# Pooled attention and a top-1 mixture of experts on one core: the turns of K and V put ahead of a unit's products with V

## The chip, the cores and the metric

The program runs on one core of one Trainium2 chip. The metric is the device time of one execution in microseconds (us). Before the change three runs took 642.44, 642.95 and 644.0 us, median 642.95. A core has five engines with a queue of its own each: TensorE (PE, with its weight loads shown as PEld), VectorE (DVE), ScalarE (ACT), GpSimd (POOL) and SyncE (SP), which starts most of the transfers.

## The reference, cut to what matters

q, k and v have 8 batches, 8 heads, 576 rows and 64 columns. K and V are averaged over groups of 8 rows, so a head has 72 pooled rows. The result of attention feeds a router and a layer of 8 experts:

```python
k_p = k.reshape(B, H, Sp, pool, D).mean(axis=3)
v_p = v.reshape(B, H, Sp, pool, D).mean(axis=3)
scores = scale * np.matmul(q, k_p.transpose(0, 1, 3, 2))
attn = softmax(scores)
x = (attn @ v_p) -> rows of 512        # 4608 rows
logits = x @ w_gate                    # 8 experts, the best one is taken
y[i] = gate_w[i] * (relu(x[i] @ w1[e]) @ w2[e])   # up to 1152 rows of each expert
```

## The kernel before, in words

The kernel has two stages. **Attention** takes up to about 193 us of the trace; a loop over pairs of row tiles through the experts follows. The change lies in attention alone.

Attention is cut into 36 **units**: 128 pairs of query rows for 4 heads at a time (`class Unit`, L438). One pass of the loop at L1011, called iteration n here (0 to 37), works on three units at once. It computes the scores of unit n (`score`, L472: `ps`), subtracts the row maximum on DVE (`softmax`, L479 and L484) and takes the exponential on ACT (`exp`, L487: `pt`). For unit n-2 it turns the exponentials in two halves on TensorE (`p_t`, L495: `pp`), copies each half on ACT (L496: `pT`) and multiplies with V (`av`, L509: `pa`), and DVE divides by the sums (`norm`, L518 to L549: `rz`, `xo`, `lt`, `lg`). For unit n+1 it turns the query rows (`q_part`, L455 and L456: `pq`, `qT`). A unit with neither of the extra works below takes some 3.6 us of TensorE.

Extra work is spread over the iterations. Two batches make a pair of nine units, and in each pair K and V of the two batches are prepared:

- **K's turn** (`prep_k`, called by `hooks` where j, the place in the pair, is 1 or 5): five transposes on TensorE (L404: `pk`), then four copies on ACT (L413) into `kbs`, about 1.75 us.
- **V's turn** (first part of `prep_v`, one iteration later): five transposes (L404) and two copies on ACT (L413) into `vT`.
- **V's product** (second part of `prep_v`, a further iteration later): twelve rows of matmuls on TensorE (L431: `pv`) with an identity and the router's weights, then two multiplications on DVE (L433 and L435) into `vbd`, the operand that `av` uses.
- **Early rows** (`transposed`, L836, iterations 31 and 32): 256 rows of the first expert are turned on TensorE (L840: `pxe`) and split into a high and a low part on ACT and DVE (L125 and L126).
- The **router's steps** (`route`, L577: `gmx`, `gd`, `gme`, `oh`, `su`, `po`, `gps` and so on) run one by one on DVE between the steps of a norm.
- POOL adds up the pooled rows of the next pairs (`tree`, L368 to L372) and later scatters row numbers (L672) and computes low parts of weights (L126).

What sets the order: every engine runs its instructions in the order in which the Python code writes them (`tc.manual_schedule`, L732). There is no planner; queues of generators (`hq` for V's preparation, `rq` for routing, `gq` and `sq` for POOL) are advanced by `step` at fixed places of the loop. `hooks(n)` stands at the end of an iteration, behind the norm.

Two facts on space matter. All small PSUM tiles (`pp`, `pq`, `pk`, `pv`, `pxe`, `po`) come from `bank` (L173), which hands out two banks in turn; a tile waits until the readers of the tile before it in its bank are done. In an iteration the order of the calls is `pp`, `pp`, `pq`, and then a turn's tile, which so takes the bank of the second `pp`. And `pa` has one buffer, so the products of a unit wait for the norm of the unit before.

Iteration 1 is special: V's turn and V's product of the first batch both stand there, with five filler matmuls (`busy`, L262) ahead of them.

Of the kernel before, what the change touches and what calls it, by code (L numbers as in the profile page):

```python
# [21 lines left out]
P = 128  # L22
KC = 96
# [8 lines left out]
def pooled_attn_top1_moe(ctx: ExitStack, tc: tile.TileContext, q, k, v, wg, w1, w2, cap, out):  # L32
# [8 lines left out]
    B, H, S, D = q.shape  # L41
    NT, DM = out.shape
    E, _, DF = w1.shape
    POOL = 8
    SP_ = S // POOL
    NCH = H * SP_ // KC
# [10 lines left out]
    NR = 9  # L57
# [66 lines left out]
    def split(hi, lo, src, eng=nc.vector):  # L124
        nc.scalar.copy(hi, src)  # L125
        eng.tensor_sub(lo, src, hi.bitcast(F32))  # L126
# [35 lines left out]
    with ExitStack() as actx:  # L162
# [10 lines left out]
        def bank(shape, name, dtype=F32):  # L173

            turn[0] ^= 1
            return ptp.tile(shape, dtype, name=name, tag=f"tp{turn[0]}")
# [45 lines left out]
        raws, qb, qtl, kps, vps, left = {}, {}, {}, {}, {}, {}  # L222
# [39 lines left out]
        def busy(n, z=None):  # L262

            z = bank([P, 512], "z") if z is None else z
            for _ in range(n):
                nc.tensor.matmul(z[:, 0:P], zw, zw, start=True, stop=True)  # L266
            return z
# [95 lines left out]
        def tree(dst, t, due=None):  # L363

            n = t.shape[1]
            t1 = kvp.tile([P, NR // 3, W // 2], F32, name="t1", tag="t1", bufs=1)[:, 0:n]
            t2 = kvp.tile([P, NR // 3, W // 4], F32, name="t2", tag="t2", bufs=1)[:, 0:n]
            nc.gpsimd.tensor_add(t1, t[:, :, 0 : W // 2], t[:, :, W // 2 :])  # L368
            yield
            nc.gpsimd.tensor_add(t2, t1[:, :, 0 : W // 4], t1[:, :, W // 4 :])  # L370
            yield
            nc.gpsimd.tensor_add(dst, t2[:, :, 0:D], t2[:, :, D:])  # L372
            if due:
                left[due] -= 1
            yield

        def red(dst, t):
            nc.vector.tensor_reduce(out=dst, in_=t.rearrange("p c (j d) -> p c d j", j=POOL), axis=AX.X, op=ALU.add)

        def pooled(p):  # L380

            kps[p] = kvp.tile([P, NR, D], F32, name="kp", tag="kp", bufs=2)
            vps[p] = kvp.tile([P, NR, D], F32, name="vp", tag="vp", bufs=2)

        def third(i):
            return slice(i * NR // 3, (i + 1) * NR // 3)

        def pool(p):
            for w, dst in (("k", kps[p]), ("v", vps[p])):
                left[w, p] = 3  # L390
                for i in range(3):
                    gq.append(tree(dst[:, third(i)], raws[p]["kv".index(w)][i], (w, p)))
# [15 lines left out]
        def natural(dst, pk):  # L408

            v = dst.rearrange("d h (g r) -> d (h g) r", r=NR)  # L410
            for o in range(2):
                n = (NR + 1 - o) // 2
                nc.scalar.copy(v[:, :, o : NR : 2], pk[o * D : (o + 1) * D, 0 : n * GB].rearrange("d (i q) -> d q i", q=GB))  # L413
# [8 lines left out]
        def prep_v(b):  # L422

            vT = wk.tile([D, H, SP_], F32, name="vT", tag="vT", bufs=1)
            natural(vT, turned(vps[b // 2], b, "v"))
            yield
            vb = vbd[b % 2]
            rows_ = vT.rearrange("d h x -> d (h x)")
            pv = bank([P, 512], "pv")[0:KC, 0 : NCH * (D + 2 * E)].rearrange("r (c x) -> r c x", c=NCH)
            for c in range(NCH):  # L430
                nc.tensor.matmul(pv[:, c], rows_[:, c * KC : (c + 1) * KC], wgi[:, c], start=True, stop=True)  # L431
            m = mk[:, :, :, None]
            nc.vector.tensor_mul(vb[:, :, :, D : D + E], pv[:, :, D:].rearrange("r c (a e) -> r c a e", a=2),  # L433
                                 m.to_broadcast([KC, NCH, 2, E]))
            nc.vector.tensor_mul(vb[:, :, :, 0:D], pv[:, :, None, 0:D].to_broadcast([KC, NCH, 2, D]), m.to_broadcast([KC, NCH, 2, D]))  # L435
            yield
# [123 lines left out]
        first, lgs, rows_out, early = {}, {}, [], {}  # L560
# [129 lines left out]
        rq, hq, aq, dq, sq, gq = [], [], [], [], [], []  # L690
# [26 lines left out]
        def step(q_, n=1):  # L717

            while q_ and n:
                if callable(q_[0]):  # L720
                    q_.pop(0)()
                    n -= 1
                elif next(q_[0], 0) == 0:
                    q_.pop(0)
                else:
                    n -= 1

        def drain(q_):
            while q_:
                step(q_)  # L730

        with tc.manual_schedule():  # L732
# [28 lines left out]
            n_early = nu - 11  # L761
# [74 lines left out]
            def transposed(i, x):  # L836

                p_ = bank([P, KD, P], "pxe", F32R)
                for c in range(KD):
                    nc.tensor.transpose(p_[:, c], x[:, i, c * P : (c + 1) * P], identr)  # L840
                s = (slice(None), slice(None), slice(i * P, (i + 1) * P))
                split(xh[s], xl[s], p_.bitcast(F32))
# [130 lines left out]

            NPU = 2 * NB + 1

            def hooks(n):

                p, j = divmod(n, NPU)
                if n == 0:
                    red(vps[0][:, NR - 1 :], raws[0][1][2][:, 2:3])  # L980
                    pooled(1)
                    pool(1)
                elif n == 1:
                    busy(5)
                    hq.append(prep_v(0))
                    drain(hq)
                if p == B // 2:
                    return
                if j == 1:
                    prep_k(2 * p + 1)  # L990
                if j == 2:
                    hq.append(prep_v(2 * p + 1))
                if p + 1 < B // 2:
                    if j == 5:
                        prep_k(2 * p + 2)
                    if j == 6:
                        hq.append(prep_v(2 * p + 2))

                if p + 2 < B // 2:
                    if j == (5 if p == 0 else 3):  # L1000
                        load_kv(p + 2)
                    if j == (7 if p == 0 else 6):
                        pooled(p + 2)
                        pool(p + 2)
                step(hq)
                if n == NB:
                    gq.append(rest)
                if n == 3 * NB:
                    setup_rows()

            for n in range(nu + 2):  # L1011
                u = units[n] if n < nu else None
                p = units[n - 2] if n > 1 else None
                nx = units[n + 1] if n + 1 < nu else None
                new = n and u and u.b != units[n - 1].b
                if new:
                    assert not aq
                    ahead(u.b)
                if n == n_start:
                    start_weights()  # L1020
                if n == n_early:
                    start_early()
                if n == n_early + 3:
                    start_ids()
                    split_early()
                if n == n_early + 4:
                    start_rows()
                if u:
                    u.score(0)
                if p:  # L1030
                    p.p_t(0)
                if u:
                    u.score(1)
                    u.softmax()
                step(aq)
                if p:
                    p.p_t(1)
                if n == nu + 1:
                    for c in range(KF):
                        nc.scalar.copy(wr["h"][:, c], wr[2][:, c])  # L1040
                if nx:
                    nx.q_part()
                flush()
                step(aq)
                if u:
                    u.exp()
                if p:
                    p.open()
                    p.av(0)
                    p.av(1)  # L1050
                step(rq, 4 if nu // 2 < n < nu - 8 else 8 if n >= nu - 8 else 0)
                step(dq)
                if p:
                    p.norm()
                    r = route_of(p)
                    if r:
                        rq.append(r)
                        if p.b == early_b - 1:
                            rq.append(favourite())
                if n_early + 6 <= n < n_early + 8:  # L1060
                    transposed(n - n_early - 6, early["x"])
                hooks(n)
                step(gq, 4 if n < n_early + 3 else max(0, min(2, n - n_early - 3)) + (n == n_start - 1))
                step(sq, 2 if n < nu - 10 else 4)
                step(aq)
# [135 lines left out]
```

## Time and profile before

| | us |
|---|---|
| runs, median (lowest to highest) | 642.95 (642.44 to 644.0) |
| the profiled execution | 645.5 |
| its span, first to last instruction | 643.8 |
| TensorE busy, weight loads | 614.2, 552.1 |
| DVE, ACT, POOL busy | 337.2, 235.0, 302.6 |
| mean granted TensorE clock | 0.991 |

A row of a timeline has the start and the duration in us, the engine, the line of the kernel, the operation, the output and its inputs, the sizes and how many instructions are merged; in brackets stands how long the engine was idle before it and whom it waited for. A row of the groups has the count, then the busy time and the mean ns of one, then the idle time before them. TensorE's rows overlap, since matmuls are pipelined; the distance of two starts is what a group takes.

### The profile page before, as it was taken

How to read it: one execution, taken by the hardware profiler on the slowest of the kernel's cores; microseconds unless marked ns; L12 is line 12 of the kernel's file. 1: busy time of each engine (PE TensorE's matmuls, PEld its weight loads, DVE VectorE, ACT ScalarE, POOL GpSimd, SP SyncE). 2: the span in 40 equal slices, each digit the busy share in tenths (PEclk: the TensorE clock that was granted, in tenths of full speed). 3: DMA queues.
4: the chain of work that ended last, by engine and by line, in shares of the span. 5: the costliest groups of instructions: out<-in, count | busy, mean ns of one | idle time of the engine just before them, and what ended most of it. 6: DMA issues, size and time to landing. Idle time of an engine off the chain costs nothing.

```text
span 643.8 us, 14831 instructions
## 1 busy us (share of the span) xinstructions
PE 614.2 (95%) x4241; PEld 552.1 (86%) x4242; DVE 337.2 (52%) x725; ACT 235.0 (36%) x398; POOL 302.6 (47%) x467
## 2 busy tenths in 40 slices
PE   9899899999979999998999999999999989999994
PEld 8789789888779889987989989988899878989983
DVE  4667878868778322267447732227422575322222
ACT  1665556557643211156235511116111462112111
POOL 7599939532953322425445532434434155441344
PEclk9999999999989999998999999999999999999998
DMA  8998744462172610227727650212712171210112
GB/s 327 356 403 280 286 156 122 169 202 96 67 290 75 228 34 33 65 90 261 274 81 280 208 185 33 65 33 95 255 49 65 51 269 36 65 49 19 63 49 65
DMA packets 47084, 93.81 MB, mean 146 GB/s; under 512 B 13392, under 2 KB 23632, under 8 KB 47060
## 3 DMA queue, kind: packets, MB, share of 16 engines
q1 hardware_dynamic: 30836, 60.37, 27.2%
q0 software_dynamic: 11392, 21.57, 11.0%
q10 hardware_dynamic: 4832, 11.56, 4.7%
q8 instruction: 14, 0.23, 0.1%
q14 instruction: 10, 0.08, 0.0%
HBM read 132.97 MB, written 31.27 MB: 255 GB/s over the span
## 4 chain that ended last, share of the span: by engine, by line
PE 83%; DVE 7%; issue 4%; ACT 2%; DVEq 2%; POOL 1%; POOLq 0%; ACTq 0%
PE y L159 29%; PE ph L150 24%; PE pa L509 7%; PE ps L472 4%; PE pp L495 3%; PE ph L1115 3%; PE pq L455 2%; PE z L266 2%; PE px L1092 2%; PE ps L150 1%; ACT kbs L413 1%; PE pv L431 1%; PE pa L159 1%; PE ps L159 1%; PE pk L404 1%
## 5 line engine op out<-in xcount | busy, mean ns | idle before, releaser
L1104 ACT ACTIVATE hh<-ph 128x512 fp32r<-128x512 f32 x60 | 35.9, 599 | 171.5 <-PE ph L150 168.4
L1105 DVE SCALAR_TENSOR_TENSOR hl<-ph,hh 128x512 fp32r<-128x512 f32 x60 | 40.9, 690 | 109.0 <-ACT hh L1104 96.7
L150 PE MATMUL ph<-xh,w1h 128*128 128x256 f32 x480 | 76.3, 281 | 1.6 <-ACT xo L957 0.8
L150 PE MATMUL ph<-xh,w1l 128*128 128x256 f32 x480 | 75.9, 280 | 0.0
L150 PE MATMUL ph<-xl,w1h 128*128 128x256 f32 x480 | 75.9, 280 | 0.0
L159 PE MATMUL y<-w2h,hh 128*128 128x512 f32 x280 | 72.5, 401 | 0.8 <-issue 0.8
L95 POOL DMA_INDIRECT xg<-xs,ix x42 | 43.9, 1046 | 56.9 <-PE y L159 49.6
L159 PE MATMUL y<-w2l,hh 128*128 128x512 f32 x280 | 69.9, 392 | 0.0
L159 PE MATMUL y<-w2h,hl 128*128 128x512 f32 x280 | 69.3, 390 | 0.0
L150 PEld LDWEIGHTS ph<-xh,w1h 128*128 128x128 f32 x480 | 65.7, 189 | 3.7 <-ACT xo L957 1.2
L509 PE MATMUL pa<-vbd,pT 96*128 96x146 f32 (+1 forms) x480 | 61.1, 290 | 4.3 <-DVE lt L535 2.6
L150 PEld LDWEIGHTS ph<-xl,w1h 128*128 128x128 f32 x480 | 65.2, 190 | 0.0
L150 PEld LDWEIGHTS ph<-xh,w1l 128*128 128x128 f32 x480 | 64.8, 189 | 0.0
L159 PEld LDWEIGHTS y<-w2l,hh 128*128 128x128 f32 x280 | 53.2, 190 | 11.3
L159 PEld LDWEIGHTS y<-w2h,hl 128*128 128x128 f32 x280 | 52.6, 188 | 10.9
L100 POOL DMA_INDIRECT out_dram<-zrow,iz x40 | 53.4, 1335 | 16.8 <-issue 14.7
L509 PEld LDWEIGHTS pa<-vbd,pT 96*128 96x128 f32 (+1 forms) x480 | 55.5, 179 | 6.4 <-DVE lt L535 3.3
L159 PEld LDWEIGHTS y<-w2h,hh 128*128 128x128 f32 x280 | 50.3, 189 | 11.1 <-issue 1.9
L126 DVE TENSOR_TENSOR xl<-px,xh 128x512 fp32r<-128x512 f32 x40 | 25.7, 685 | 60.5 <-ACT xh L125 60.5
L93 POOL TENSOR_TENSOR guard<-ix 128x2 int32<-128x2 int32 x21 | 5.5, 263 | 101.6 <-DVE ix L90 85.9
L672 POOL DMA_INDIRECT slots<-pairs,gix x36 | 35.3, 981 | 30.2 <-DVE pairs L665 10.8
L496 ACT COPY pT<-pp 96x384 f32<-96x384 f32 x72 | 34.1, 475 | 39.8 <-PE pp L495 34.5
(234 smaller groups left out, 1050.0 us busy)
## 6 DMA issues: line engine op xcount, KB each, us to landing
r<-in_moe_w_dram SPq DMA_DIRECT2D x84, 1024.0 KB
raw<-in_k_dram SPq DMA_DIRECT2D x12, 768.0 KB
raw<-in_v_dram SPq DMA_DIRECT2D x12, 768.0 KB
xs<-xo ACTq DMA_DIRECT2D x16, 512.0 KB
qblk<-in_q_dram SPq DMA_DIRECT2D x14, 512.0 KB
raw<-in_moe_w_dram SPq DMA_DIRECT2D x4, 512.0 KB
r<-in_moe_w_dram ACTq DMA_DIRECT2D x2, 1024.0 KB
qblk<-in_q_dram SPq DMA_DIRECT2D x4, 256.0 KB
```

What stands on the lines that cost most here:

```text
L95: nc.gpsimd.indirect_dma_start(out=dst[:, i, :].bitcast(F32), out_offset=None, in_=src, in_offset=bass.IndirectOffsetOnAxis(ap=ix[:, i, 0: ...
L100: ins = nc.gpsimd.indirect_dma_start(out=out[:, :], out_offset=bass.IndirectOffsetOnAxis(ap=i_, axis=0), in_=src, in_offset=None, bounds_c ...
L126: eng.tensor_sub(lo, src, hi.bitcast(F32))
L150: nc.tensor.matmul(p[:, f2], a[:, c, f * P : (f + 1) * P], b[:, c], start=(f2 == 0 and j == 0 and c == 0), stop=(f2 == 1 and j == 2 and c ...
L159: nc.tensor.matmul(y, a[:, c, i * P : (i + 1) * P], b[:, c], start=(n == 0), stop=(n == 3 * KF - 1))
L472: nc.tensor.matmul(self.ps[:, h, 0 : 2 * SP_].rearrange("p (a x) -> p a x", a=2), self.qT[:, h], kbs[self.b % 2][:, :, self.hf * HH + h], ...
L495: nc.tensor.transpose(pp[0:KC, c], self.pt[:, (j * HC + c) * KC : (j * HC + c + 1) * KC], ident)
L496: nc.scalar.copy(self.pT[:, j], pp[0:KC, 0:HC])
L509: nc.tensor.matmul(self.pa[us, j, h0 * XW : (h0 + 2) * XW], self.pT[:, j, c, us], vbd[b % 2][:, cc].rearrange("r a x -> r (a x)"), start=( ...
L672: ins = nc.gpsimd.indirect_dma_start(out=slots[:, :], out_offset=bass.IndirectOffsetOnAxis(ap=ix[:, g, 0:1], axis=0), in_=pairs[:, pr + g0 ...
L1104: nc.scalar.activation(hh[s], p, AF.Relu)
L1105: nc.vector.scalar_tensor_tensor(out=hl[s], in0=p, scalar=0.0, in1=hh[s].bitcast(F32), op0=ALU.max, op1=ALU.subtract)
```

## The change

A new function `turns(n)` takes K's turn, V's turn, V's product and the early rows out of the end of the iteration (out of `hooks`, behind the norm) and puts them between the exponential and the products with V. Loads and POOL's work stay in `hooks`. In iteration 1 the fillers and V's turn go ahead of the exponential, and four more fillers go ahead of V's first product, into its bank.

```diff
@@ prep_v
-            pv = bank([P, 512], "pv")[0:KC, 0 : NCH * (D + 2 * E)].rearrange("r (c x) -> r c x", c=NCH)
+            pv = bank([P, 512], "pv")
+            if b == 0:
+                busy(4, pv)
+            pv = pv[0:KC, 0 : NCH * (D + 2 * E)].rearrange("r (c x) -> r c x", c=NCH)
@@ the loop's helpers
-            def hooks(n):
+            def turns(n):
 
                 p, j = divmod(n, NPU)
-                if n == 0:
-                    red(vps[0][:, NR - 1 :], raws[0][1][2][:, 2:3])
-                    pooled(1)
-                    pool(1)
-                elif n == 1:
-                    busy(5)
-                    hq.append(prep_v(0))
+                if n == 1:
                     drain(hq)
+                if n_early + 6 <= n < n_early + 8:
+                    transposed(n - n_early - 6, early["x"])
                 if p == B // 2:
                     return
                 if j == 1:
...
                         prep_k(2 * p + 2)
                     if j == 6:
                         hq.append(prep_v(2 * p + 2))
-
+                step(hq)
+
+            def hooks(n):
+
+                p, j = divmod(n, NPU)
+                if n == 0:
+                    red(vps[0][:, NR - 1 :], raws[0][1][2][:, 2:3])
+                    pooled(1)
+                    pool(1)
+                if p == B // 2:
+                    return
                 if p + 2 < B // 2:
...
-                step(hq)
                 if n == NB:
@@ the loop
                 step(aq)
+                if n == 1:
+                    busy(5)
+                    hq.append(prep_v(0))
+                    step(hq)
                 if u:
                     u.exp()
+                turns(n)
                 if p:
                     p.open()
                     p.av(0)
...
-                if n_early + 6 <= n < n_early + 8:
-                    transposed(n - n_early - 6, early["x"])
                 hooks(n)
```

Line numbers of the changed kernel are higher by 3 from `prep_v`'s matmuls to `hooks`, and more behind it. TensorE, iterations 10 and 11, K's turn and V's turn. Before (`pa` is the product with V, `ps` the scores, `pp` the turned weights):

```order
L455 MATMUL pq<-identr,qblk 128x128 x4
L509 MATMUL pa<-vbd_149,pT 128x146 x6
L404 MATMUL pk<-identr,kp 128x64 x4
L404 MATMUL pk<-identr,kp 64x64
L472 MATMUL ps<-kbs_146,qT 128x144 x2
L495 MATMUL pp<-identr,pt 96x128 x3
L472 MATMUL ps<-kbs_146,qT 128x144 x2
L495 MATMUL pp<-identr,pt 96x128 x3
L455 MATMUL pq<-identr,qblk 128x128 x4
L509 MATMUL pa<-vbd_148,pT 128x146 x6
L404 MATMUL pk<-identr,vp 128x64 x4
L404 MATMUL pk<-identr,vp 64x64
```

And now:

```order
L458 MATMUL pq<-identr,qblk 128x128 x4
L404 MATMUL pk<-identr,kp 128x64 x4
L404 MATMUL pk<-identr,kp 64x64
L512 MATMUL pa<-vbd_149,pT 128x146 x6
L475 MATMUL ps<-kbs_146,qT 128x144 x2
L498 MATMUL pp<-identr,pt 96x128 x3
L475 MATMUL ps<-kbs_146,qT 128x144 x2
L498 MATMUL pp<-identr,pt 96x128 x3
L458 MATMUL pq<-identr,qblk 128x128 x4
L404 MATMUL pk<-identr,vp 128x64 x4
L404 MATMUL pk<-identr,vp 64x64
L512 MATMUL pa<-vbd_148,pT 128x146 x6
```

Each turn has moved ahead of the products with V of its own iteration. DVE, iteration 12, where V's product is multiplied into `vbd` and routing steps (`oh`, `su`) stand among the norm. Before:

```order
L484 TENSOR_TENSOR pt<-ps,mx 128x4x2x72
L518 TENSOR_SCALAR rz<-pa 128x8
L610 TENSOR_TENSOR oh_180<-cw,gmm 128x8
L520 RECIPROCAL rz<-rz 128x8
L614 TENSOR_REDUCE su<-oh_180 128x80
L534 TENSOR_TENSOR xo<-pa,rz 128x2x256
L535 TENSOR_TENSOR lt<-pa,rz 128x2x32
L621 TENSOR_REDUCE oh_181<-oh_180 128x8
L549 TENSOR_REDUCE lg<-lt 128x16
L433 TENSOR_TENSOR vbd_149<-pv,mk 96x12x8
L435 TENSOR_TENSOR vbd_149<-pv,mk 96x12x64
L479 TENSOR_REDUCE mx<-ps 128x8
```

And now:

```order
L487 TENSOR_TENSOR pt<-ps,mx 128x4x2x72
L436 TENSOR_TENSOR vbd_149<-pv,mk 96x12x8
L438 TENSOR_TENSOR vbd_149<-pv,mk 96x12x64
L521 TENSOR_SCALAR rz<-pa 128x8
L613 TENSOR_TENSOR oh_180<-cw,gmm 128x8
L523 RECIPROCAL rz<-rz 128x8
L617 TENSOR_REDUCE su<-oh_180 128x80
L537 TENSOR_TENSOR xo<-pa,rz 128x2x256
L538 TENSOR_TENSOR lt<-pa,rz 128x2x32
L624 TENSOR_REDUCE oh_181<-oh_180 128x8
L552 TENSOR_REDUCE lg<-lt 128x16
L482 TENSOR_REDUCE mx<-ps 128x8
```

The two multiplications have moved from behind the norm to ahead of it. DVE, iteration 31, the split of the early rows (`xl`). Before:

```order
L484 TENSOR_TENSOR pt<-ps,mx 128x4x2x72
L518 TENSOR_SCALAR rz<-pa 128x8
L520 RECIPROCAL rz<-rz 128x8
L534 TENSOR_TENSOR xo<-pa,rz 128x2x256
L535 TENSOR_TENSOR lt<-pa,rz 128x2x32
L126 TENSOR_TENSOR xl<-pxe,xh 128x4x128
```

And now:

```order
L487 TENSOR_TENSOR pt<-ps,mx 128x4x2x72
L126 TENSOR_TENSOR xl<-pxe,xh 128x4x128
L521 TENSOR_SCALAR rz<-pa 128x8
L523 RECIPROCAL rz<-rz 128x8
L537 TENSOR_TENSOR xo<-pa,rz 128x2x256
L538 TENSOR_TENSOR lt<-pa,rz 128x2x32
```

The split has moved ahead of the norm here as well. On POOL and SP the order is the same in both kernels. On ACT it differs at two places: in iteration 1 `vT`'s copies stand ahead of the exponential, and in iteration 29 they stand ahead of a routing exponential.

## The prediction

> **What bounds the kernel now.** I read the page first, then the list of waits of TensorE from 0 to 220 us (who waited for what: total, times, longest), then the timeline. Page:
>
> ```profile
> PE 614.2 (95%) x4241; PEld 552.1 (86%) x4242; DVE 337.2 (52%) x725; ACT 235.0 (36%) x398; POOL 302.6 (47%) x467
> ```
>
> TensorE is busy 95% of the span. The edit lies in attention, up to about 193 us; later code only starts earlier or later. So only TensorE's waits in attention can be won:
>
> ```profile
> PE pa L509 <- DVE lt L535: 2.6, 3, 2.0
> PE pp L495 <- DVE vbd L435: 2.4, 4, 1.1
> PE pp L495 <- ACT kbs L413: 1.9, 6, 0.3
> PE pv L431 <- ACT vT L413: 1.2, 1, 1.2
> ```
>
> Lines 2 to 4 are waits for a turn's readers: 5.5 us, the ceiling of a simple gain. "Iteration n" is a pass of the loop at L1011; its products with V are those of unit n-2. Iteration 10 (K) and 11 (V):
>
> ```profile
> 62.52 0.48 ACT L496 COPY pT<-pp 96x384 f32<-96x384 f32 x1 [0.29 <-PE pp L495]
> 62.77 1.66 PE L509 MATMUL pa<-vbd,pT 96*128 96x146 f32 x12
> 63.84 0.68 ACT L487 ACTIVATE pt<-pt 128x576 f32<-128x576 f32 x1 [0.23 <-DVE pt L484]
> 64.36 0.52 PE L404 MATMUL pk<-identr,kp 64*128 64x64 f32 x5
> 64.81 0.76 PE L472 MATMUL ps<-kbs,qT 128*128 128x144 f32 x4
> 64.92 1.75 ACT L413 COPY kbs<-pk 64x320 f32<-64x320 f32 x4 [0.39 <-PE pk L404]
> 65.73 0.66 PE L472 MATMUL ps<-kbs,qT 128*128 128x144 f32 x4
> 66.72 0.53 PE L495 MATMUL pp<-identr,pt 128*96 128x128 f32 x3 [0.33 <-ACT kbs L413]
> 67.71 1.66 PE L509 MATMUL pa<-vbd,pT 96*128 96x146 f32 x12
> 69.30 0.51 PE L404 MATMUL pk<-identr,vp 64*128 64x64 f32 x5
> 69.74 0.76 PE L472 MATMUL ps<-kbs,qT 128*128 128x144 f32 x4
> ```
>
> The four copies end at 66.67 and the second turn of the next unit's weights (pp) waits for that, in the same PSUM bank.
>
> **The change part by part.** No matmul but four fillers is added, no DMA moves, and the order on POOL and SP is the same; on ACT the turn's copies stood right behind the exponential already. What moves is TensorE's order and, with it, DVE's.
>
> *K's turn, iterations 10, 14, 19, 23, 28.* The turn takes the bank that the second pp has just left, so it now waits for pT's copy: 62.52 + 0.48 = 63.00, about 63.03 with the release, where TensorE was free at 62.77: **0.27 lost**. The turn takes 0.45 (64.36 to 64.81), so the products start at 63.48 and, taking 1.59 (62.77 to 64.36), leave TensorE to the next scores at 65.07. The exponential ends at 64.52, so the copies start 0.38 earlier and end at 66.28; pp is due at 66.38 and no longer waits. The two pT copies of iteration 11 end near 67.3, V's turn starts there instead of the products, and the scores of iteration 12 come at 67.35 + 0.45 + 1.59 = 69.39 against 69.74: **-0.35**. I take -0.35 four times, and -0.2 at 28, where I judge the copies' own wait smaller. Ends: 0 (ACT's chain hides it) and -0.5.
>
> *Iterations 5 and 6.*
>
> ```profile
> 45.50 0.66 PE L455 MATMUL pq<-identr,qblk 128*128 128x128 f32 x4
> 46.09 1.72 PE L509 MATMUL pa<-vbd,pT 96*64 96x146 f32 x24
> 46.31 0.59 POOL L372 TENSOR_TENSOR vp<-t 128x192 f32<-128x192 f32 x1
> 47.73 0.52 PE L404 MATMUL pk<-identr,vp 64*128 64x64 f32 x5
> ```
>
> V's turn would be ready near 46.0 now, but POOL writes the last third of its pooled rows until 46.90. Behind it stand the products: 46.96 + 0.45 + 1.64 (46.09 to 47.73) = 49.05 for the next scores, against 47.73 + 0.45 = 48.18: **+0.9**. Ends: +0.3, if V's rows come in time, and +1.2. As POOL's time does not hang on TensorE, this swallows whatever iterations 1 to 4 win or lose: there
>
> ```profile
> 22.31 0.68 ACT L487 ACTIVATE pt<-pt 128x576 f32<-128x576 f32 x1 [0.57 <-DVE pt L484]
> 22.90 0.84 ACT L413 COPY vT<-pk 64x320 f32<-64x320 f32 x2
> ```
>
> vT's copies no longer follow the exponential (-0.24), and two bank waits come (+0.54). If POOL were earlier than I read, those 0.3 stay instead of 0.9.
>
> *Products of V, iterations 7, 12, 16, 21, 25, 30.* Each takes a bank wait of 0.27 and frees the bank before the next pp needs it. At 7 that is even. At 16 and 25 I see no wait to win: **+0.27 each**. At 12 and 21 DVE is late, because of the routing steps among its work:
>
> ```profile
> 68.67 1.81 POOL L368 TENSOR_TENSOR t<-raw 128x768 f32<-128x768 f32 x1
> 69.49 1.09 DVE L591 TENSOR_TENSOR gd<-lg,gmx 128x72 f32<-128x72 f32 x1
> 72.17 0.21 DVE L535 TENSOR_TENSOR lt<-pa,rz 128x64 f32<-128x64 f32 x1
> 74.00 0.74 DVE L484 TENSOR_TENSOR pt<-ps,mx 128x576 f32<-128x576 f32 x1
> 74.12 1.24 PE L431 MATMUL pv<-wgi,vT 64*96 64x80 f32 x12
> 75.30 0.71 PE L469 MATMUL ps<-kbs,qT 128*64 128x144 f32 x8
> 76.97 0.25 DVE L433 TENSOR_TENSOR vbd<-pv,mk 96x96 f32<-96x96 f32 x1
> 77.14 0.95 DVE L435 TENSOR_TENSOR vbd<-pv,mk 96x768 f32<-96x768 f32 x1
> 78.23 0.50 PE L495 MATMUL pp<-identr,pt 128*96 128x128 f32 x3 [1.12 <-DVE vbd L435]
> 79.01 0.67 PE L509 MATMUL pa<-vbd,pT 96*128 96x146 f32 x4
> ```
>
> TensorE arrives about 0.6 late (0.9 - 0.35). gd ends at 70.58, 0.10 behind POOL's tree step at 70.48: DVE's step waits for POOL here, whose clock is its own, so part of the lag is absorbed. V's products then run 72.6 to 73.8 while the norm of iteration 11 ends, the products with V 73.8 to 75.3, the scores at 75.4. DVE multiplies vbd at 75.3 to 76.5, while TensorE works, not at 76.97 to 78.09; pp at about 77.1 does not wait. The products of iteration 13 then stand behind the norm, about 78.25 against 79.01. From +0.6 to -0.75: **-1.35**; ends -0.4 and -1.7. The Trainium skill, "SBUF — State Buffer", section "Who interferes with whom", says that a DVE instruction with two SBUF inputs is fully blocked by a GpSimd instruction that reads SBUF and came first; the trace agrees (70.58 against 70.48). Were these long steps DVE's own length instead, the lag would not be absorbed: -0.75 here, and 641.0 for the whole.
>
> Iteration 21 is of the same kind and smaller:
>
> ```profile
> 120.34 0.50 PE L495 MATMUL pp<-identr,pt 128*96 128x128 f32 x3 [0.46 <-DVE vbd L435]
> ```
>
> 0.46 of wait, and V's products fill the wait for the norm: **-0.8** (ends 0 and -1.2). At 30 both are weaker: **-0.3** (0.3 to -0.6).
>
> *Early rows, iterations 31 and 32.* Their split on DVE now stands ahead of the norm, which waits for ACT's cast; the norm of 32 and all routing behind it come about 1 us later. It is hidden at the end of attention:
>
> ```profile
> 175.31 3.73 POOL L126 TENSOR_TENSOR w1l<-raw,w1h 128x512 fp32r<-128x512 f32 x3
> 176.65 2.45 DVE L648 TENSOR_TENSOR gps<-gps,oh 128x32 f32<-128x32 f32 x1
> 179.88 1.39 PE L509 MATMUL pa<-vbd,pT 96*128 96x146 f32 x9 [2.00 <-DVE lt L535]
> ```
>
> gps waits for POOL until 179.04 whether it starts at 176.65 or 177.7, and POOL's chain is tied to ACT's casts of iteration 30. **0**; without that cover +1.0.
>
> **Sum:** +0.9 - 1.4 - 0.2 + 0.54 - 1.35 - 0.8 - 0.3 = **-2.6 us**. The profiled execution took 645.5 (span 643.8, 1.7 around it), so 642.9 there; the median of the runs shown is 642.95, 2.55 below the profiled one, so **640.4**.
>
> **The rivals.** *A, the waits only change their name:* the bank waits come at every turn, and DVE gives nothing at 12, 21 and 30 (0.27 lost at the first two, even at the third): +0.9 - 1.6 + 0.54 + 0.54 = +0.4, 643.3. For it: TensorE is busy 95%, and pT's copy stands in front of every moved turn. Against it: the 1.12 at 78.23 has a plain cause that goes. *B, slower: the norm stands behind vbd's multiplications.* pa has one buffer, so a unit's products wait for the norm of the unit before; where DVE has no idle time before the norm, 0.25 + 0.94 = 1.19 stand ahead of it. At 12, 21 and 30 together 3.57, on the +0.9 - 1.6 + 0.54 that remain: +3.4, 646.4. It decides from where DVE is still busy when the products end.
>
> ```profile
> L518 DVE TENSOR_SCALAR rz<-pa 128x8 f32<-128x8 f32 x36 | 5.8, 162 | 23.3 <-PE pa L509 18.2 <-PE pk L404 2.1 <-issue 1.8
> ```
>
> Against it: the norm's first step idled 18.2 us for the products, 0.5 per unit, so there is usually room. *C, a larger gain: gps no longer meets POOL.* The 2.0 us wait at 179.88 goes, and with it the slow clock behind it (PEclk is the column before the last two):
>
> ```profile
> 182.00:184.00 2.00, 2.00 (x11) 1.95 (x11) 1.12 (x5) 0.73 (x2) 1.49 (x3) 0.50 0.88 261
> ```
>
> 2 us at half speed are 1.0 more: 640.4 - 3.0 = 637.4. Against it: gps must come 1.3 us earlier against POOL, and the split of the early rows makes it later.
>
> **How the numbers follow.** Forecast 0.50, A 0.28, B 0.12, C 0.10. A measurement of this kernel tells 0.3% (1.9 us) from no change: faster is below 641.0, slower above 644.9. The forecast is only 0.6 below that bound; with the ends of its terms I give 0.40 of its 0.50 to faster. Faster 0.40 + 0.10 = 0.50, same 0.10 + 0.28 = 0.38, slower 0.12. The forecast's own range is 638.8 to 642.3. The range asked for reaches into A and to the near side of C: 638.3 to 644.2.
>
> **What would show it.** Right: the wait of pp for kbs and vbd gone from the list of waits; new waits of pk and pv for pT of about 0.27; one wait of pk for POOL's vp near 46 us of about 1 us; V's products ending before pa's at 12 and 21; the products of iteration 34 still behind gps and POOL. Wrong: no wait for vp near 46; pa waiting longer for lt than the 2.6 of now; gps at its short length.

## The result, and the profile after

On the chip of the first comparison the changed kernel took 648.12 us (median of 6 runs, 647.39 to 650.01) against 643.04 us (640.99 to 644.0) of the kernel before: ratio 1.0074, 95% interval 1.0055 to 1.0094. That is 5.1 us slower, where 2.6 less had been forecast, and outside the range. On another chip, in the last experiments, the same kernel measured 0.9991 (0.9968 to 1.0014). So much is taken ahead: the loss comes from a place behind the change where VectorE (DVE) and POOL meet, and against the kernel before it shows on one chip and not on the other.

The profiled execution after took 647.39 us, the lowest of its six runs; its span is 645.6. The profile before (645.5) lies 2.5 above its median. So the two profiles differ by 1.8 us in span, and some 3 of the 5.1 us between the medians can't be seen in them. The page has TensorE's work nearly as before:

```profile
PE 614.5 (95%) x4249; PEld 553.0 (86%) x4250; DVE 340.0 (53%) x725; ACT 234.4 (36%) x398; POOL 302.2 (47%) x467
```

DVE has grown by 2.8 us with the same 725 instructions. The list of waits, 0 to 220 us (total, times, longest):

```profile
PE po L637 <- DVE su L617: 4.9, 2, 4.4
PE pa L512 <- DVE lt L538: 1.8, 2, 1.0
PE pk L404 <- POOL vp L372: 1.4, 1, 1.4
PE pk L404 <- ACT pT L499: 1.0, 5, 0.2
PE pp L498 <- DVE vbd L438: 0.6, 1, 0.6
```

The waits for `kbs` are gone, as forecast; those for `vbd`, forecast to go too, have shrunk from 2.4 to 0.6. At the top stands a wait that was not in the forecast: the router's `po` for `su`, 4.4 us at once. Where time was lost or won is seen from the starts of the first scores of an iteration in the two timelines (the last row is the first matmul of the first expert):

| iteration | before | after | after - before |
|---|---|---|---|
| 0 | 17.02 | 16.18 | -0.84 |
| 6 | 43.09 | 43.18 | +0.09 |
| 7 | 48.18 | 49.44 | +1.26 |
| 12 | 69.74 | 70.69 | +0.95 |
| 14 | 81.21 | 81.90 | +0.69 |
| 21 | 111.81 | 112.22 | +0.41 |
| 23 | 122.61 | 122.29 | -0.32 |
| 28 | 145.02 | 143.70 | -1.32 |
| 33 | 170.30 | 169.56 | -0.74 |
| 34 | 175.54 | 179.36 | +3.82 |
| expert | 193.06 | 194.66 | +1.60 |

The 0.84 at iteration 0 stands ahead of everything that was changed. At iteration 33 the changed kernel was 0.74 ahead. One iteration then cost 4.56. Of these, 2.2 come back up to the first expert, since the kernel before has its own wait of 2.00 for the norm one iteration later, with half clock behind it. The timeline of the changed kernel there:

```profile
173.97 3.97 DVE L594 TENSOR_TENSOR gd<-lg,gmx 128x32 f32<-128x32 f32 x1
174.18 3.70 POOL L126 TENSOR_TENSOR w1l<-raw,w1h 128x512 fp32r<-128x512 f32 x3
179.12 0.38 PE L637 MATMUL po<-su,matr 128*128 128x8 f32 x1 [4.36 <-DVE su L617]
```

And of the kernel before:

```profile
173.85 0.18 DVE L591 TENSOR_TENSOR gd<-lg,gmx 128x32 f32<-128x32 f32 x1
```

The routing step `gd` took 3.97 us in place of 0.18: it ended as POOL's three splits did (174.18 + 3.70 = 177.88). Before, the splits began at 175.31, behind `gd`, and held `gps`, behind which stands the norm that TensorE waits for later. Now `su` and `po` stood behind `gd`, and TensorE had nothing to do. The windows of the changed kernel show it; behind the length stand busy us and count of PE, PEld, DVE, ACT and POOL, then the granted clock, DMA's share and GB/s:

```profile
174.00:176.00 2.00, 0.77 (x11) 0.48 (x7) 2.00 (x2) 0.69 (x1) 1.97 (x3) 1.00 0.63 240
176.00:178.00 2.00, 0.00 (x0) 0.00 (x0) 1.97 (x2) 0.03 (x1) 1.92 (x3) 0.53 0.00 0
178.00:180.00 2.00, 0.88 (x4) 0.88 (x5) 1.50 (x9) 0.20 (x1) 1.10 (x2) 0.50 0.39 65
180.00:182.00 2.00, 2.00 (x10) 1.94 (x10) 1.00 (x4) 0.47 (x1) 0.00 (x0) 0.50 1.03 393
182.00:184.00 2.00, 2.00 (x15) 1.94 (x14) 1.70 (x6) 0.96 (x2) 0.00 (x0) 0.77 0.87 269
```

TensorE idles from 175 to 179, and its clock is granted at half from 176 until 183. This is the theory for the experiments: **the meeting of `gd` with the splits, and the half clock behind it, make the change slow; the order of the turns alone is about even.** The rival: the order of the turns itself costs the time, and the meeting only shows where.

### The profile page after: what moved, and what is told of

It is laid out like the page before. It is cut to its first block, busy times and chain, and to the rows that moved or that the text cites. A ratio compares the mean times of both kernels' runs of the same rounds, so it can differ in the third digit from the quotient of the medians.

```text
span 645.6 us, 14845 instructions
## 1 busy us (share of the span) xinstructions
PE 614.5 (95%) x4249; PEld 553.0 (86%) x4250; DVE 340.0 (53%) x725; ACT 234.4 (36%) x398; POOL 302.2 (47%) x467
## 4 chain that ended last, share of the span: by engine, by line
PE 59%; DVEq 2%; issue 2%; DVE 1%; POOL 1%; ACT 1%; POOLq 0%; ACTq 0%
PE y L159 30%; PE ph L150 24%; PE ph L1126 3%; PE px L1103 2%; PE ph L1136 1%; ACT w2h L125 1%; DVEq L1154 0%; DVEq L1153 0%; POOL out_dram L100 0%; DVE w2l L126 0%; DVEq L1152 0%; DVE hs L1128 0%; DVE hl L1116 0%; DVEq L1148 0%; DVEq L1149 0%
```

## The experiments

Each ratio is to the kernel before, run beside it on the same chip; the kernel before itself had medians from 643.8 to 652.7 us there.

### One: the splits taken out of the way, and the early rows alone

In two kernels the scatters of iterations 30 to 32 are held back, so that POOL's splits come 2.3 us (changed) and 5.0 us (before) earlier and are over, or nearly, when DVE reaches the routing:

```diff
-                step(sq, 2 if n < nu - 10 else 4)
+                step(sq, 2 if n < nu - 10 else 0 if 30 <= n < 33 else 4)
```

The changed kernel with it:

> The changed kernel, with POOL's scatters of row numbers held back in iterations 30 to 32 (they follow from iteration 33), so that the last three low parts of weights (w1l) are computed some microseconds earlier and no longer lie across the routing steps of iteration 33. Theory 1 (the loss is the collision of gd with POOL's w1l and the slow clock behind it): gd takes under 1 us instead of 3.97, the wait of po for su falls from 4.4 us to under 1, the clock stays at 1.0, and the kernel takes 641 to 643.5. Theory 2 (the order of the turns itself loses, spread over attention): 646 or more.

The kernel before with it:

> The kernel before, with the same scatters held back. Theory 1: gps no longer takes 2.45 us and the products of iteration 34 do not wait 2.0 us; 2 to 3 us are won where the kernel before meets this collision in most executions (640 to 641), nothing where the profiled execution was an exception (643). Theory 2: no difference by itself, 643.

In two more the early rows alone change place, in the changed kernel back behind the norm, in the kernel before ahead of the products:

> The changed kernel, with the early rows alone back behind the norm (iterations 31 and 32). Theory 1a (the early rows ahead of the norm delay the routing of iteration 33 so that gd meets POOL): gd comes about 1 us earlier against POOL's triple, it misses it, and gps meets it as before: 643 to 644.5. Theory 1b (POOL's triple came earlier because V's product of iteration 30 moved): gd still meets it, 647 to 648.

> The kernel before, with the early rows alone ahead of the products with V. Theory 1a: the routing of iteration 33 meets POOL with gd, or with a step ahead of po, and the kernel loses 3 to 5 us: 646 to 648. Theory 1b: POOL's triple stays where it was, gps meets it as before, 643 to 644.

| kernel | ratio | 95% interval |
|---|---|---|
| changed, held | 0.9994 | 0.9977 to 1.0012 |
| before, held | 0.9964 | 0.9948 to 0.998 |
| changed, early rows back | 1.0069 | 1.0043 to 1.0095 |
| before, early rows ahead | 0.9989 | 0.9972 to 1.0005 |

The early rows are not the cause: with them back the changed kernel is as slow, since the splits then hold another step of the same chain:

```profile
173.56 4.21 DVE L610 TENSOR_TENSOR oh<-cw,gmm 128x32 fp32r<-128x32 f32 x1
174.01 3.71 POOL L126 TENSOR_TENSOR w1l<-raw,w1h 128x512 fp32r<-128x512 f32 x3
```

With them ahead the kernel before keeps its meeting at `gps`, longer than its 2.45, and the time stays:

```profile
174.56 3.46 DVE L648 TENSOR_TENSOR gps<-gps,oh 128x32 f32<-128x32 f32 x1
```

With the hold the changed kernel stands at 0.9994 (1.0074 in the first comparison; it was not run without the hold on this chip), the kernel before at 0.9964; the times, 643.85 and 641.63, lie 0.3 and 0.6 above what the first theory gave. That speaks for the meeting, but 0.3% (2 us) between the two orders stayed. The spans of the two profiles differ by 3.0, and 1.85 of these come at one place, where the changed kernel with the hold ran at half clock and the kernel before with it did not. Changed, held, and then before, held:

```profile
82.00:84.00 2.00, 2.00 (x11) 0.50 0.94 363
```

```profile
82.00:84.00 2.00, 2.00 (x19) 1.00 0.95 343
```

The first comparison's profile of the changed kernel had no half clock there, so this is not a cost that every execution pays. The ten runs fit that: with a mean granted clock of 0.993 or more (four runs) the changed kernel with the hold took 641.6 to 642.2 us, with 0.991 or less (six runs) 643.8 to 645.5; the kernel before with the hold has a median of 641.6. So most of the 2 us goes with the clock. What sets the clock off at 82 was not tried.

### Two: which turns, with the hold

Four kernels choose by a list in which iterations the turns stand ahead of the products; in all others they stand behind the norm, and the hold is in all. Iteration 1 is as in the kernel before, without the four new fillers.

```diff
-                turns(n)
+                if n in EARLY:
+                    turns(n)
...
+                if n not in EARLY:
+                    turns(n)
                 hooks(n)
```

> The scatters of iterations 30 to 32 are held in this and the next three kernels, so the meeting of gd with POOL's last triple is out of all of them; the kernel before with that hold measured 0.9964 of the kernel before, the changed kernel with it 0.9994. The two differ by the order of the turns alone, some 2 us. Here K's and V's own turns (iterations 5, 6, 10, 11, 14, 15, 19, 20, 23, 24, 28, 29) stand ahead of the products with V; V's products and the early item's rows stand behind the norm. Theory (the table of iteration starts of the two profiles carries over): +1.5 at 5 and 6 from the wait for POOL's vp, -0.25 to -0.35 at each later pair, together about +0.4 us on the kernel before with the hold, 0.997 of the kernel before. Rival (K's and V's turns carry the whole 2 us, their gains being those of one profile): 0.9995 or above.

> Only the products of V (iterations 3, 7, 12, 16, 21, 25, 30) stand ahead of the unit's products with V; all else stands as before, with the hold. Theory by the table: +0.28 each at 3, 7, 16 and 25 for the wait on a bank, -0.26 at 12, -0.73 at 21, nothing at 30: about 0 us, 0.9960 to 0.9970. Rival (the two SBUF operands of the early item's routing meet POOL's tree again at 12 and 13, as in the changed kernel's profile, and what vbd's multiplications gain is lost): +1 to +2 us, 0.998 to 0.9995.

> Only the early item's rows (iterations 31 and 32) stand ahead of the unit's products with V, with the hold. Theory (their transposes stand ahead of the unit's products and its norm, su and po come later, TensorE idles longer in front of po and its clock is granted at half behind it, as the changed kernel with the hold showed from 178 to 180): +1 to +2.5 us on the kernel before with the hold, 0.998 to 1.000, with a dip of the clock at 178 to 182. Rival (the early rows are even; the kernel before with them early and without the hold measured 0.9989): 0.9960 to 0.9970 and no dip.

> The turns stand ahead of the products with V only in iterations 10 to 12, 14, 15, 19 to 21, 23 and 24, where the table of iteration starts of the two profiles shows gains; the wait for POOL's vp at 5 and 6, the bank waits at 3, 7, 16 and 25 and the early rows stay as before; with the hold. Theory (the gains are real): -0.35 at each of four pairs, -0.73 at 21, -0.26 at 12: about -2 us on the kernel before with the hold, 0.993 to 0.994. Rival (POOL sets the pace of these iterations, so that what TensorE gains is waited off later): 0.996 to 0.997.

They measured 1.0186 (1.0104 to 1.0268), 1.0321 (1.0268 to 1.0373), 1.021 (1.0142 to 1.0277) and 1.0192 (1.0121 to 1.0262), all far from every expectation. In all four ACT stood still for 13.2 us and DVE for 8 to 11, near the time 180. So the kernel before with the hold was run again as a control, on a third chip, with three of the four:

> The kernel before with the scatters of iterations 30 to 32 held, once more, as the control of the next three. In the last four kernels ScalarE and VectorE stood still for 10 to 13 us near the time 180 with their operands ready, in front of the 4 MB that load the first expert's weights; the kernel before did not lose that time beside them. Theory (the hold, which sets those loads some 4 us earlier, puts an instruction load behind them on that chip, whatever the order of the turns): if this call shows such a stall at all, this kernel shows it too, 1.02 of the kernel before; if it shows none, 0.995 to 0.998 as the first time. Rival (the order of the turns brings it): 0.995 to 0.998 here, and 1.02 in the next three.

> The turns ahead of the products with V only in iterations 10 to 12, 14, 15, 19 to 21, 23 and 24, with the hold. Up to the time 178 its first profile ran 0.46 us ahead of the kernel before with the hold, where the table of iterations said 2. Theory (the gains are real but POOL and DVE's waits take most back): 0.5 us less than the control of this call, ratio 0.9955 to 0.9965 if there is no stall. Rival (gains in full): 0.993 to 0.994.

> K's and V's own turns alone ahead of the products with V, with the hold. Its first profile stood 1.2 us behind the kernel before with the hold at the time 178. Theory (the wait for POOL's vp at 5 and 6 and little back later): 0.4 to 1.2 us more than the control of this call, 0.997 to 0.9985. Rival (these turns carry all of the 2 us between the two orders): 2 us or more over the control, 0.9995 or above.

> V's products alone ahead of the unit's products with V, with the hold. In its first profile the lag on the kernel before with the hold was 3.5 us at iteration 25 and 5 at 26, from stalls in which ScalarE and VectorE waited with their operands ready. Theory (those stalls are an instruction load's and not the order's): without them within 0.5 us of the control of this call, 0.996 to 0.997. Rival (the products set those stalls off by where they stand): 3 us or more over the control, 1.001 or above.

The control, 0.9964 on the chip of experiment one, measured 1.0214 (1.0164 to 1.0264) here, the others 1.0244 (1.0222 to 1.0267), 1.0253 (1.0209 to 1.0297) and 1.0278 (1.0236 to 1.0319). So the hold brings the loss, not the order, and only on some chips. The waits of the control, 170 to 215 us; "remote" means that nothing in the profile released the instruction:

```profile
ACT pT L496 <- remote: 13.2, 1, 13.2
DVE rz L518 <- remote: 9.8, 1, 9.8
```

ACT and DVE stood still with their operands ready. The hold lets the splits end earlier, and the 4 MB of loads that wait for them start earlier too: SP issues the first at 175.53 here and at 174.05 on the chip of experiment one, against 179.07 in the kernel before. One packet of the queue for instructions landed at 182 to 184 on the chip of experiment one (first row) and only at 194 to 196 here (second row; packets, MB, share):

```profile
q14 instruction: 1, 0.01, 1.0%
```

```profile
q14 instruction: 1, 0.01, 1.1%
```

The expectations read this as an instruction load queued behind the weights. The trace of the control does not bear it out: its packet starts at 195.37, after ACT had gone on at 194.36 and DVE at 190.04, and from 171 until then no instruction packet is seen. So the late packet follows the standstill, and what caused that stays open. For the order of the turns these eight runs say this much: in the profiles, up to iteration 34, the products of V alone stood 2.6 us behind the control, K's and V's turns alone 0.4 ahead, the mixed choice 0.3 behind. Of the 2.6, 1.8 came in iteration 24, where ACT's copies of `kbs` began 1.8 us after their operands were ready; the first run of this kernel lost 3.7 there, and no other profile did. So the rival of that expectation, that the place of V's products sets such a standstill off, is not ruled out. The gain of 2 us that the table above promised for the mixed choice did not come.

### Three: the splits one scatter later, or one earlier

One scatter is 1.27 us of POOL. The changed kernel gets five ahead of the splits in place of four, the kernel before gets three:

```diff
-                step(sq, 2 if n < nu - 10 else 4)
+                step(sq, 2 if n < nu - 10 else 5 if n == n_start - 2 else 4)
```

> The changed kernel with one more scatter (1.27 us of POOL) ahead of its last three splits, so that they start near 175.4 instead of 174.2, behind gd at 174.0. Theory (the meeting of gd with the splits costs the time): gd takes 0.18 us again, the gps multiplication near 176.7 waits some 2.4 us for the splits, as in the kernel before, and the time is 3 to 4 us under the changed kernel's: 0.9995 to 1.002 of the kernel before. Rival (the order of the turns costs it, wherever the splits stand): 1.006 to 1.009, as the changed kernel.

> The kernel before with one scatter fewer ahead of the last three splits, so that they start near 174.0 instead of 175.3, on top of gd and the two steps behind it. Theory: one of gd, gme and oh takes 3 to 4 us, TensorE idles in front of po and then runs at half clock, and the time is 3 to 4.5 us over the kernel before: 1.004 to 1.007, without any change in the order of the turns. Rival: within 0.2 per cent of the kernel before.

The changed kernel with five: 1.0003 (0.9977 to 1.0029). The kernel before with three: 1.0066 (1.0031 to 1.01). Both are what the theory said, and the rivals' numbers lie outside. The changed kernel with five scatters; `gd` is short, `gps` is held, and the products with V wait for it as they did in the kernel before:

```profile
174.57 0.18 DVE L594 TENSOR_TENSOR gd<-lg,gmx 128x32 f32<-128x32 f32 x1
176.04 3.71 POOL L126 TENSOR_TENSOR w1l<-raw,w1h 128x512 fp32r<-128x512 f32 x3
177.54 2.27 DVE L651 TENSOR_TENSOR gps<-gps,oh 128x32 f32<-128x32 f32 x1
180.60 1.76 PE L512 MATMUL pa<-vbd,pT 96*128 96x146 f32 x12 [1.99 <-DVE lt L538]
```

The kernel before with three, without any change in the order of the turns:

```profile
174.57 3.91 DVE L591 TENSOR_TENSOR gd<-lg,gmx 128x32 f32<-128x32 f32 x1
174.69 3.73 POOL L126 TENSOR_TENSOR w1l<-raw,w1h 128x512 fp32r<-128x512 f32 x3
179.66 0.27 PE L634 MATMUL po<-su,matr 128*128 128x8 f32 x1 [3.14 <-DVE su L614]
```

```profile
182.00:184.00 2.00, 2.00 (x11) 0.50 0.82 260
```

It is the same meeting, with an idle TensorE (3.14 us) and half clock behind it. In two more kernels, both with five scatters, one of the three splits goes into the iteration ahead as well, so that only two are left at the end:

```diff
-                step(gq, 4 if n < n_early + 3 else max(0, min(2, n - n_early - 3)) + (n == n_start - 1))
+                step(gq, 4 if n < n_early + 3 else max(0, min(2, n - n_early - 3)) + (n == n_start - 2))
```

> The kernel before with five scatters in place of four and three splits in place of two in the iteration ahead, so that only two splits remain and start near 177.8, behind the gps multiplication at 176.65. The first expert's loads start some 1.3 us later than in the kernel before, not 4 us earlier. Theory (a kernel with no meeting saves what the hold saved on the first chip, and the instruction loads are not set behind the weights): 0.9955 to 0.998 on any chip. Rivals: the one split more at iteration 31 meets something else, 0.999 to 1.001; the loads hit the instruction loads all the same, 1.02.

> The same edit on the changed kernel: its last two splits would start near 176.7, beside the gps multiplication at about 176.75, which they hold up to 2.4 us or miss. Theory: gd and oh pass in 0.2 us, and the time is 3 to 5 us under the changed kernel's, 0.998 to 1.002; what then remains over the kernel before with this edit (0 to 2.5 us) is what the order of the turns costs by itself. Rival (the order of the turns costs all): 1.006 or above.

The kernel before with it measured 1.0024 (0.9997 to 1.0051), not the gain that was expected; the changed kernel 0.9974 (0.994 to 1.0007). In the profile of the first, `gd` passes in 0.18, but DVE then stands still, and `gps` comes 2.2 us later than in the kernel before:

```profile
178.56 0.17 DVE L518 TENSOR_SCALAR rz<-pa 128x8 f32<-128x8 f32 x1 [3.40 <-remote]
178.88 1.18 DVE L648 TENSOR_TENSOR gps<-gps,oh 128x32 f32<-128x32 f32 x1
```

Its clock is then granted at half from 182 to 186. That is a standstill of the kind that the hold met, here without a large load under way (the first is issued at 180.03). What sets it off stays open. With this edit the changed kernel is 0.5% below the kernel before, with the hold it was 0.3% above, and with five scatters level. The three pairs differ in sign, so no steady cost of the order by itself comes out of them.

### Four: the changed kernel on a further chip, and the turns of the second half alone

> The changed kernel itself once more, for the step from it to the kernel with one scatter more. Theory: the meeting of gd with the splits is there again on this chip (gd near 4 us) and the time is 1.005 to 1.009 of the kernel before. Rival (the meeting was of one chip's timing): 0.998 to 1.003.

The last kernel is the changed one with five scatters, with the turns of iterations 1 to 13 behind the norm as before (the list of experiment two holds 14 to 32):

> The changed kernel with one scatter more ahead of the last splits, and with the turns up to iteration 13 behind the norm as in the kernel before; from 14 on they stand ahead of the products with V. Theory (POOL's multiplications at 13 and 14 wipe out what lies ahead of them, so that the terms at 5, 6, 12 and 13 count for little, and the later gains of some 1.4 us reach the end when gd is free): 0.997 to 0.9995. Rival (nothing is left of the gains): 1.000 to 1.003.

The changed kernel measured 0.9991 (0.9968 to 1.0014), 652.36 us against 652.73 of the kernel before. The meeting is there:

```profile
175.20 3.94 DVE L594 TENSOR_TENSOR gd<-lg,gmx 128x32 f32<-128x32 f32 x1
```

So the rival's reason falls though its number came. On this chip the kernel before is 7 to 10 us slower than on the others. Its runs there have a lower granted clock (median 0.98, against 0.99 on the chip of experiment three); it was not profiled there, and why is open. The other kernel measured 0.9912 (0.9883 to 0.9941), 647.29 us, below what was expected: it beats both kernels on this chip, its `gd` taking

```profile
174.67 0.18 DVE L592 TENSOR_TENSOR gd<-lg,gmx 128x32 f32<-128x32 f32 x1
```

It was not run on another chip, so the 0.9912 says little on the order of the turns. Most of its 5 us under the changed kernel is again the price of the meeting: at iteration 34 the two profiles are 4.4 us apart, after 0.5 at 33.

## Why the prediction was wrong, step by step

**Early rows and the end of attention, forecast 0, was +4.56 at iteration 33: the step that failed.** The forecast let DVE come later against POOL and found that `gps` waits until 179.04 anyway. It did not let POOL come earlier. Its own sentence, that POOL's chain is tied to ACT's casts of iteration 30, held the answer: the gains up to iteration 30 (-1.38 there) move POOL's chain with them, while the iterations 31 and 32 give 0.6 back to DVE's side. POOL's row in iteration 30, before and after:

```profile
162.97 1.01 POOL L672 DMA_INDIRECT slots<-pairs,gix  x1 [0.16 <-issue]
```

```profile
161.84 1.00 POOL L675 DMA_INDIRECT slots<-pairs,gix  x1 [0.74 <-DVE rz L523]
```

The casts and the two splits behind them came 1.71 earlier (158.56 after 160.27); the scatter then waited 0.74 for DVE's routing, of which two steps (`ghi`) took 0.80 and 1.23 beside those splits in place of 0.17 each. From there POOL runs without a pause: 1.13 earlier here, 1.13 earlier at the splits (175.31 to 174.18). `gd` came 0.12 later (173.85 to 173.97). A distance of 1.46 between `gd` and the splits became 0.21, and that was near enough: `gd`'s row begins 0.21 ahead of the splits and is held all the same (0.12 and 0.18 ahead in the other two profiles with this meeting). Why POOL did not wait instead is open. `gps` itself took 0.19 in the changed kernel, at 179.76, so the cover that the forecast counted on was gone. Experiment three shows this as cause in both directions. The Trainium skill, "SBUF — State Buffer", section "Who interferes with whom", has the rule for it (a DVE instruction with two SBUF inputs contends with a GpSimd instruction that reads SBUF); the runs agree: `gd` 0.18 alone, 3.91 to 3.97 beside the splits. The forecast had used that rule only for a lag that POOL absorbs, never for a step that a gain would bring into it.

**Iterations 12 and 13, forecast -1.35, was -0.26.** The multiplications of `vbd` did move to 75.25, and the second turn of weights (77.66) no longer waits. But the norm behind them was held:

```profile
75.42 0.94 DVE L438 TENSOR_TENSOR vbd<-pv,mk 96x768 f32<-96x768 f32 x1
76.28 1.81 POOL L368 TENSOR_TENSOR t<-raw 128x768 f32<-128x768 f32 x1
76.35 1.76 DVE L613 TENSOR_TENSOR oh<-cw,gmm 128x8 fp32r<-128x8 f32 x1
77.66 0.53 PE L498 MATMUL pp<-identr,pt 128*96 128x128 f32 x3
79.60 1.64 PE L512 MATMUL pa<-vbd,pT 96*128 96x146 f32 x11 [0.96 <-DVE lt L538]
```

`oh` stands between the first two steps of the norm and took 0.35 before. The step that failed is "the products of iteration 13 then stand behind the norm, about 78.25": they came at 79.60. Rival B had the place right, a norm behind `vbd`, but priced it at the 1.19 of the multiplications, not at POOL's step. In seven of the ten profiles with `vbd` early `oh` takes 1.75 to 1.76 and the tree step starts 0.07 to 0.08 ahead of it, so this meeting is no accident of one execution; why they keep that distance was not tried. In one of the other three (changed, early rows back) `oh` passed in 0.15, and the lag fell from +2.03 at 12 to +0.55 at 14, by 1.48, about what was forecast. That fits the meeting as what took the gain.

**Iterations 5 and 6, forecast +0.9, was +1.26** (the scores of iteration 7 at 49.44, forecast 49.05). The mechanism was right, the size too small: POOL wrote its rows until 46.90 + 0.59 = 47.49 here, 0.59 later than in the kernel before, on whose 46.90 the forecast was built as if it stood still. It does not: the same step starts at 46.04 to 46.92 in the six profiles with the kernel before's turns throughout, its early rows aside.

```profile
46.90 0.59 POOL L372 TENSOR_TENSOR vp<-t 128x192 f32<-128x192 f32 x1
47.54 0.33 PE L404 MATMUL pk<-identr,vp 64*128 64x64 f32 x2 [1.45 <-POOL vp L372]
```

Little of that loss reaches the end. Of the nineteen other profiles, all but two reach iteration 14 within about 0.7 us of the kernel before's first profile, wherever between -0.4 and +2.6 they stood at 11. That fits POOL's steps holding DVE at 12 and 13; it was not tried by itself.

**What held.** The bank wait of 0.27 came at each turn that was named for it (1.0 in five waits on `pT`, and +0.28 in the starts at 3, 7 and 16; at 25 the kernel before had a wait of 0.47 for `vT`'s copies that the forecast did not see, and the change gave -0.56 in place of +0.27). The pairs from 10, 14, 19 and 23 gave -0.21 to -0.33 each, somewhat less than the -0.35 of the forecast, and the pair from 28 gave -0.05 in place of -0.2. Iteration 21 and the one behind it gave -0.73 (from +0.41 to -0.32) where -0.8 was forecast; iteration 30 gave nothing (+0.05) in place of -0.3. The routing at the end did stay behind POOL, only another step of it.

**The sum.** From iteration 14 to 33 the change won 1.4 us in the profile, where the terms add up to 1.8, but in part by luck: the gain at 25 that was not forecast made up for what the pairs and 30 did not give and for the 0.6 that iterations 31 and 32 took back. With the meeting out of the way by one scatter, the changed kernel is level with the kernel before (1.0003, 1.7 us either way, on one chip), not 2.6 below it. So even a right guess of the meeting would have given "no difference", nearest to rival A's number, for another reason than A's.

## What to carry to other kernels

A gain of one microsecond moves every engine that hangs on the gaining one, and the engines that do not hang on it stay: before a time is forecast, list the pairs of DVE and POOL steps that pass each other by less than the expected shift, in both directions, and price the meeting by its longest step and by who stands behind the held instruction. A forecast of -2.6 us is worth little beside a distance of 1.46 us between two such steps, one of which costs 4 us when they meet. And an experiment that moves a collision out of the way should move it by the smallest step (one scatter), since a larger one moves transfers too.

## What the runs showed of the hardware

- **Standing still with operands ready.** When 4 MB of loads were issued 3.5 us earlier than in the kernel before (175.53 against 179.07), ACT stood still for 13.2 us and DVE for 9.8; the same program, with the loads at 174.05, did not stand still on another chip. The packet of the instruction queue that comes late (195.37) starts only after both had gone on; the cause is open.
- **The same wait, two clocks.** A wait of about 2 us in front of the products with V (2.00 in the kernel before, 1.99 in the changed kernel with five scatters, 1.92 in the last kernel) was followed by half clock in the first and the last and by full clock in the second.
- **The chip matters more than the change.** The kernel before had medians of 643.0, 643.8, 645.8, 644.7, 646.1 and 652.7 us (the fourth and fifth on one chip), and one and the same edit, the hold, measured 0.9964 on one chip and 1.0214 on another.
